# Transposing a second batch at full width: 96-row loads, copies and a new order in an attention and feed-forward kernel

## The chip, the cores and the metric

The kernel runs on one core of a Trainium2 chip. The metric is the device time of one execution in microseconds (us); less is better. Times shown are medians over executions, with their lowest and highest.

The core has a matrix engine (TensorE, PE in the profile, with its weight loads listed as PEld), a vector engine (VectorE, DVE), a scalar engine for activation functions (ScalarE, ACT), a general engine (GpSimd, POOL) and a queue engine (SyncE, SP). Matmuls read SBUF and write PSUM; a matmul holds one operand as weights in the array and streams the columns of the other through it. DMAs are issued from the queues of SP, ACT and POOL.

## The reference

```python
# q, k, v: [8 batches, 8 heads, 576, 64], f32; moe_w_in: [512, 2048]; moe_w_out: [2048, 512]
scores = (1 / sqrt(64)) * q @ k.transpose(0, 1, 3, 2)
mask = abs(pos[:, None] - pos[None, :]) <= 32
scores = where(mask, scores, -1e9)
attn = exp(scores - max(scores, -1))
attn = attn / (sum(attn, -1) + 1e-09)
x = (attn @ v).transpose(0, 2, 1, 3).reshape(8 * 576, 512)
h = x @ moe_w_in
out = maximum(0.01 * h, h) @ moe_w_out        # [4608, 512], f32
```

## The kernel before

The attention is cut into 64 steps. Step i belongs to batch b = i // 8, to half hf = (i // 4) % 2 of its 576 positions (288 each) and to a pair p = i % 4 of heads, whose 2 x 64 dimensions stand on the 128 partitions. A step is a set of scores (`score`: five matmuls into the one PSUM tile `ps`), an exponential on ACT (`exps`, tile `e`), the multiplication with the band mask (`masked`, tile `prob`, on POOL or DVE), the sums over keys (`sums`: matmuls with a block of ones, tile `s`), the reciprocal of the sums (`inverse`, a DVE instruction, tile `r`), the product with the values (`product`, tile `x`), and the scaling (`scaled`) into `xT`, the input of the feed-forward part. `sums` and `product` share a PSUM pool with one buffer for each of their tiles.

The feed-forward part goes by groups g of 288 positions: for each of 16 slices f of the hidden width `h_mms` makes four matmuls with `w_in_bf`, and ACT writes the leaky result to `gT` (`h_out`). For each 128 positions `o_tile` makes 16 matmuls of 512 columns with `w_out_bf`, in four groups of four with a hook before each; ACT copies the result out of PSUM and SP stores it.

The order on every engine is the order in which the program calls these functions (`manual_schedule`). The prologue, by hand, does steps 0 to 7 (batch 0) among the first feed-forward tiles. Then the loop at the end goes through a plan of hidden and output tiles; before each piece `spend` counts a turn, runs what the table `SECOND` lists for that turn, and later the steps that are due. `SECOND` covers batch 1's first half (steps 8 to 11) and the preparation of batch 2; turns 1 to 16 are the four groups of the first four output tiles.

What the change touches:

- Loading. `load_first` loads two heads side by side with a cast to bf16 onto 128 rows: 64 rows for each head of the pair, 9 positions of 64 in each row. It is used for batch 0 and, four times with two pairs each, for batch 1, issued from POOL's queue into `qb` and `kb`. POOL's queue also carries the weights (`load_w_in`, `load_w_out`, 512 KB each as bf16), batch 1's values (`load_v`), and in between POOL's own masks of steps 4, 5 and 6. A DMA on this queue waits for the one issued eight before it. The f32 loads of later batches (`load_qk`, tiles `qf` and `kf`, all pairs in `q_in` and `k_in`) go by SP.
- Transposing. For batches 0 and 1 `transpose_first` turns each head alone: 9 x 2 transposes of 64x64 into a PSUM tile `tp`, two quarters of the array at a time. `evict_first` copies `tp` to `qT` or `kT` on ACT or DVE; for the keys `place_keys` copies `kT` to block-diagonal `kbd` (two DVE copies). From batch 2 on, POOL casts the f32 rows (`cast_qk`) and a DMA transposes (`transpose_dma`); in the table these are `turned`. PSUM tiles `tp`, the hidden tiles and the output tiles share a pool of four buffers.
- Reciprocals. Steps 0 to 3 (`NEWTON`) do not use `inverse` but ACT's logarithm (`log_of`), ACT's exponential of its negative (`guess`), and one correction on DVE (`missed`, `mended`); `scaled` then takes the sign into account.

Of the kernel before, what the change touches and what calls it, by code (L numbers as in the profile page):

```python
# [10 lines left out]
BF16 = mybir.dt.bfloat16  # L11
# [5 lines left out]
def kernel(  # L17
# [14 lines left out]
    nc = tc.nc  # L32

    B, H, S, D = q.shape
# [5 lines left out]
    NPAIR = H // 2  # L40
# [17 lines left out]
    mmps = ctx.enter_context(tc.tile_pool(name="mmps", bufs=4, space=PS))  # L58
# [5 lines left out]
    RUN = S // 96  # L64
# [3 lines left out]
    q_in = fload.tile([128, H * RUN * D], FP32, name="qf")  # L68
    k_in = fload.tile([128, H * RUN * D], FP32, name="kf")

    def load_qk(b, p, behind=None):

        for into, src, t in ((qf, q, q_in), (kf, k, k_in)):
            t = t[0:96].rearrange("p (n a e) -> p n a e", n=NPAIR, a=2)[:, p]
            if behind is not None:
                behind.memset(t[0:1, 0, 0:1], 0.0)
                behind = None
            heads = src[b, 2 * p:2 * p + 2]
            nc.sync.dma_start(
                out=t.rearrange("p a (g e) -> p a g e", g=3),  # L80
                in_=heads.rearrange("a (g p c) d -> p a g (c d)", g=3, c=2),
            )
            into[b, p] = t

    ROW = S // 64
    qb_t = const.tile([128, NPAIR, RUN * 2 * D], BF16, name="qb")
    kb_t = const.tile([128, NPAIR, RUN * 2 * D], BF16, name="kb")
    qb, kb = (
        t[0:96].rearrange("i p (c a d) -> i p c a d", c=RUN, a=2) for t in (qb_t, kb_t)
    )  # L90
    q0b, k0b = (
        t[:, :, 0:ROW * D].rearrange("i p (c d) -> i p c d", c=ROW)
        for t in (qb_t, kb_t)
    )

    def load_first(b, p, which, n=1):

        src, to = ((q, q0b), (k, k0b))[which == "k"]
        nc.gpsimd.dma_start(
            out=to[:, p:p + n].rearrange("i p c d -> i p (c d)"),  # L100
            in_=src[b, 2 * p:2 * (p + n)].rearrange("(p a) (i c) d -> (a i) p (c d)", a=2, c=ROW),
        )
# [5 lines left out]
    def load_v(b, p, engs=(nc.sync, nc.sync)):  # L108
# [14 lines left out]
    ident = const.tile([128, 128], BF16)  # L123
# [6 lines left out]
        out=band, in_=band, compare_op=ALU.is_ge, fill=0.0,  # L130
# [3 lines left out]
        out=band, in_=band, compare_op=ALU.is_ge, fill=0.0,  # L134
# [16 lines left out]
    def copy_to(eng, out, in_):  # L151
        if eng is nc.scalar:
            eng.activation(out=out, in_=in_, func=AF.Copy)
        else:
            eng.tensor_copy(out=out, in_=in_)
# [45 lines left out]
    trans, kTs = {}, {}  # L201

    def transpose_first(b, p, which):

        src = (q0b, k0b)[which == "k"]
        tp = mmps.tile([128, ROW, 64], BF16, name="tp", tag="mm")
        for c in range(ROW):
            for r in HEADS:
                nc.tensor.transpose(tp[r, c], src[r, p, c], ident[r, r])  # L209
        trans[b, p, which] = tp.rearrange("p c i -> p i c")  # L210

    def evict_first(b, p, which, eng):
        if which == "q":
            if b not in qT:
                qT[b] = attn.tile([128, NPAIR, S], BF16, name="qT")
            to = qT[b][:, p]
        else:
            to = kTs[b, p] = kt.tile([128, S], BF16, name="kT")
        copy_to(eng, to.rearrange("p (i c) -> p i c", c=ROW), trans.pop((b, p, which)))

    def value_first(a, eng):
        r = HEADS[a]
# [29 lines left out]
    def place_keys():  # L252

        while landing and landing[0][0] <= state["done"]:
            unplaced.append(landing.pop(0)[1:])
        while unplaced:
            b, p, kT = unplaced.pop(0)
            for a in range(2):
                r = slice(64 * a, 64 * a + 64)
                to = kbd[b % 2][r, p, :, r]  # L260
                if b < NATURAL:
                    nc.vector.tensor_copy(out=to, in_=kT[r].rearrange("p (n j) -> p n j", j=64))
                    continue
                nc.vector.tensor_copy(  # L264
                    out=to.rearrange("p n (m c) -> p n c m", c=2),
                    in_=kT[r].rearrange("p (c n m) -> p n c m", c=2, n=NB),
                )
# [4 lines left out]
    def where(i):  # L272
        return i // 8, (i // 4) % 2, i % 4
# [43 lines left out]
    def masked(i, eng):  # L317
        b, hf, p = where(i)
        e = probs[i]
        pr = prob[:, i % NPROB]  # L320
        allowed = mask_first[hf] if b < NATURAL else mask[hf].rearrange("p n c i -> p n (c i)")
        eng.tensor_mul(  # L322
            pr.rearrange("p n c i -> p n (c i)"), e.rearrange("p (n t) -> p n t", n=2), allowed,
        )
        probs[i] = [pr, None, None, None]
# [9 lines left out]
    def sums(i, spare=False):  # L335

        b, hf, p = where(i)
        pr, both = probs[i][:2]
        if spare:
            s = mmps.tile([128, 512], FP32, name="mm", tag="mm")[:, 0:HALF]  # L340
        else:
            s = xps.tile([128, HALF], FP32, name="s")
        if both is not None:
            nc.tensor.matmul(s, ones_bd, both, start=True, stop=True)  # L344
        else:
            for n in range(2):
                nc.tensor.matmul(  # L347
                    s, ones_bd, pr[:, n].rearrange("p c i -> p (c i)"),
                    start=(n == 0), stop=(n == 1),
                )  # L350
        probs[i][2] = s
        if b > 0:
            inverse(i)

    def inverse(i):
        r = recip.tile([128, HALF], FP32, name="r")
        nc.vector.reciprocal(r, probs[i][2])  # L357
        probs[i][2] = r
# [10 lines left out]
    def missed(i):  # L369
        r = recip.tile([128, HALF], FP32, name="r")  # L370
        nc.vector.tensor_mul(r, probs[i][2], guesses[i])  # L371
        probs[i][2] = r
# [7 lines left out]
    def product(i):  # L380

        b, hf, p = where(i)
        pr = probs[i][0]
        x = xps.tile([128, HALF], FP32, name="x")
        x_v = x.rearrange("p (c i) -> p c i", c=2)
        flat = pr.rearrange("p n c i -> p n (c i)")
        parts = [(n_, *block) for n_ in range(2) for block in WIN[hf][n_]]
        for n_, blk, i0, n in parts:
            lo, hi = 2 * i0, 2 * (i0 + n)
            nc.tensor.matmul(  # L390
                x[:, lo:hi] if b < NATURAL else x_v[:, :, i0:i0 + n], vbd[b % 2][:, p, blk, :],
                flat[:, n_, lo:hi] if b < NATURAL else pr[:, n_, :, i0:i0 + n],
                start=(blk == parts[0][1]), stop=(blk == parts[-1][1]),
                skip_group_check=True,
            )
        probs[i][3] = x
# [4 lines left out]
        t0 = (b * S + hf * HALF) % RING  # L401
        return xT[:, p, t0:t0 + HALF]

    NEWTON = (0, 1, 2, 3,)

    def scaled(i):
        r, x = probs.pop(i)[2:]
        if i in NEWTON:
            nc.vector.scalar_tensor_tensor(  # L409
# [42 lines left out]
    def h_close(f):  # L452
        h_out(0, f, opened.pop(f))
# [99 lines left out]
    def load_w_out(i):  # L553
        c = slice(4 * i, 4 * i + 4)
        nc.gpsimd.dma_start(out=w_out_bf[:, c, :], in_=w_out_r[:, c, :])

    V, G, A = nc.vector, nc.gpsimd, nc.scalar
# [16 lines left out]
    exps(0)  # L574
    transpose_first(0, 1, "q")
    evict_first(0, 1, "k", A)
    masked(0, V)
    load_v(0, 2, (G, G))
# [56 lines left out]
    guess(3)  # L635
    h_chunk(1)
    masked(4, G)
    missed(3)
    score(5)
    product(3)  # L640
# [1 line left out]
    exps(5)  # L642
    h_chunk(2)
    scaled(3)
    load_w_out(3)
    sums(4)
    h_chunk(3)
    inverse(4)
    masked(5, G)
    product(4)  # L650
    h_close(0)
    score(6)
# [5 lines left out]
    h_close(2)  # L658
    sums(5)
    masked(6, G)  # L660
    load_first(1, 0, "k", 2)
    load_first(1, 0, "q", 2)
    load_first(1, 2, "k", 2)
    load_first(1, 2, "q", 2)
    score(7)
    h_close(4)
    inverse(5)
# [44 lines left out]
    for p in range(NPAIR):  # L712
        load_v(1, p, (G, G))
    for p in range(NPAIR):
        load_qk(2, p, G if p == 0 else None)

    def second_keys(p, eng):
        transpose_first(1, p, "k")
        evict_first(1, p, "k", eng)
        unplaced.append((1, p, kTs[1, p]))  # L720
        place_keys()

    def second_queries(p, eng):
        transpose_first(1, p, "q")
        evict_first(1, p, "q", eng)

    def finish(i):
# [3 lines left out]
    def turned(p):  # L731
        cast_qk(2, p)
        transpose_dma(2, p)

    SECOND = {
        1: [(second_keys, 0, A), (second_keys, 1, V)],
        3: [(second_queries, 0, A), (second_queries, 1, V)],
        4: [(second_keys, 2, A)],
        5: [(score, 8), (second_keys, 3, A)],
        6: [(score, 9)],  # L740
        7: [(sums, 8), (second_queries, 2, A), (second_queries, 3, A)],
        8: [(score, 10)],
        9: [(finish, 8), (sums, 9)],
        10: [(score, 11), (turned, 0)],
        11: [(finish, 9)],
        12: [(sums, 10), (turned, 1)],
        13: [(finish, 10)],
        14: [(score, 12), (turned, 2)],
        15: [(sums, 11)],
        16: [(finish, 11), (join, 12), (score, 13), (turned, 3)]  # L750
        + [(load_v, 2, p) for p in range(NPAIR)],
    }
    state["done"] = 12


# [11 lines left out]
    at, t = {}, 0.0  # L767
# [57 lines left out]
```

## Time and profile before

| | us |
|---|---|
| median of 3 runs | 315.47 |
| lowest, highest | 314.63, 315.93 |
| the profiled execution | 314.2 |
| its span | 312.5 |
| PE busy in the span | 304.2 |
| DVE, ACT, POOL busy | 218.7, 171.4, 177.9 |

The span is what the profile covers of the profiled execution; the rest lies around it. The granted PE clock is full in the whole span. Line numbers such as L209 are those of the kernel before, printed above. A row of the timeline reads: start, length, engine, line, operation, output<-input, shape, count, and in brackets the idle time before it with what ended it. PE's ends are modelled, and some matmul records are missing, so a group's time on PE is best read from its start to the start of the next group.

### The profile page before, as it was taken

The numbers are of one execution on the slowest core, as the hardware profiler recorded it, in microseconds if no ns is written. First come the engines' busy times: TensorE is split into PE (matmuls) and PEld (weight loads), VectorE is DVE, ScalarE is ACT, GpSimd is POOL, SyncE is SP. The second block draws the span as 40 slices with busy tenths as digits, with TensorE's granted clock in tenths as the row PEclk, the third lists the DMA queues.
The fourth block names the chain that finished last, engine by engine and source line by source line (L and its number), as shares of the span: only waits on it lengthen the run. The fifth ranks groups of instructions, "written<-read, shape, count | busy, mean of one in ns | idle before, by whom it ended". The sixth has DMA issues, their size and how long they took to land.

```text
span 312.5 us, 6890 instructions
## 1 busy us (share of the span) xinstructions
PE 304.2 (97%) x2662; PEld 205.7 (66%) x2683; DVE 218.7 (70%) x281; ACT 171.4 (55%) x380; POOL 177.9 (57%) x246
## 2 busy tenths in 40 slices
PE   5999999999999999999999999999999999999996
PEld 4777755776757667675856768585755858576753
DVE  6698588899557986699647996698665997665100
ACT  4775844664735556382825738283743828373531
POOL 8988625624648765686557855786456866330000
PEclk9999999999999999999999999999999999999999
DMA  7999999979999994699719994499627410000102
GB/s 123 171 199 207 206 188 226 218 139 225 227 181 213 244 196 103 157 222 171 157 42 212 213 216 112 115 224 222 141 63 126 109 56 34 36 35 5 65 30 73
DMA packets 107313, 46.09 MB, mean 147 GB/s; under 512 B 68752, under 2 KB 102800, under 8 KB 107280
## 3 DMA queue, kind: packets, MB, share of 16 engines
q1 hardware_dynamic: 91936, 37.91, 61.7%
q0 software_dynamic: 14752, 7.59, 18.3%
q8 instruction: 21, 0.34, 0.5%
q10 hardware_dynamic: 592, 0.15, 0.2%
q14 instruction: 12, 0.10, 0.1%
HBM read 36.70 MB, written 9.44 MB: 148 GB/s over the span
## 4 chain that ended last, share of the span: by engine, by line
PE 94%; DVE 2%; DMA 1%; issue 1%; ACT 1%; POOL 0%; DVEq 0%; ACTq 0%; POOLq 0%
PE mm L485 40%; PE mm L427 39%; PE x L390 5%; PE ps L303 4%; PE tp L209 2%; PE s L344 2%; DMA qb<-in_q_dram 1%; PE s L347 1%; PE ps L286 1%; DVE r L357 1%; PE ps L295 1%; DVE r L376 1%; DVE xT L409 0%; DVE r L371 0%; ACT e L314 0%
## 5 line engine op out<-in xcount | busy, mean ns | idle before, releaser
L357 DVE RECIPROCAL r<-s 128x288 f32<-128x288 f32 x60 | 117.4, 1956 | 52.3 <-PE s L344 50.3
L427 PE MATMUL mm<-xT,w_in_bf 128*128 128x288 bf16 x1024 | 133.8, 286 | 0.6 <-DVE xT L413 0.4
L485 PE MATMUL mm<-w_out_bf,gT 128*128 128x512 bf16 (+2 forms) x571 | 129.8, 373 | 1.2 <-issue 0.2
L438 ACT ACTIVATE gT<-mm 128x288 bf16<-128x288 f32 x256 | 101.7, 411 | 25.5 <-PE mm L427 8.9
L427 PEld LDWEIGHTS <-w_in_bf 128*128 128x128 bf16 x1024 | 98.5, 98 | 25.4 <-issue 1.2
L322 POOL TENSOR_TENSOR prob<-e,mask 128x576 bf16<-128x576 bf16 x48 | 61.2, 1274 | 84.3 <-issue 43.8
L485 PEld LDWEIGHTS <-gT 128*128 128x128 bf16 x592 | 55.9, 98 | 57.7
L490 ACT ACTIVATE o_sb<-mm 128x512 f32<-128x512 f32 (+2 forms) x37 | 21.7, 586 | 90.3 <-PE mm L485 87.2
L314 ACT ACTIVATE e<-ps 128x576 bf16<-128x576 f32 x64 | 41.4, 647 | 13.8 <-PE ps L303 7.4
L237 POOL CAST vbd<-vf 64x576 bf16<-64x576 f32 x48 | 32.8, 683 | 1.4
L264 DVE COPY kbd<-kT 64x576 bf16<-64x576 bf16 x48 | 32.4, 675 | 0.3
L413 DVE TENSOR_TENSOR xT<-x,r 128x288 bf16<-128x288 f32 x60 | 27.5, 458 | 6.4 <-DVE r L357 0.5
L232 POOL CAST kb<-kf 96x384 bf16<-96x384 f32 x48 | 27.5, 597 | 0.6 <-DMA kf<-in_k_dram 0.6
L232 POOL CAST qb<-qf 96x384 bf16<-96x384 f32 x48 | 24.6, 540 | 4.7 <-DMA qf<-in_q_dram 4.7
L390 PE MATMUL x<-prob,vbd 128*128 128x128 bf16 (+2 forms) x320 | 26.0, 213 | 0.0
L390 PEld LDWEIGHTS <-vbd 128*128 128x128 bf16 x320 | 20.3, 98 | 2.9
L332 DVE TENSOR_TENSOR both<-prob 128x288 bf16<-128x288 bf16 x52 | 19.8, 380 | 0.8
L303 PEld LDWEIGHTS <-kbd 128*128 128x128 bf16 x240 | 15.5, 98 | 6.7
L303 PE MATMUL ps<-qT,kbd 128*128 128x128 bf16 (+2 forms) x240 | 19.3, 211 | 0.0
L344 PE MATMUL s<-both,ones_bd 128*128 128x288 bf16 x52 | 14.9, 286 | 0.0
L115 POOL DMA_DIRECT2D vbd<-in_v_dram x14 | 10.4, 757 | 4.7 <-DMA kb<-in_k_dram 2.2
L322 DVE TENSOR_TENSOR prob<-e,wide 128x576 bf16<-128x576 bf16 x12 | 5.8, 485 | 4.1 <-ACT e L314 4.0
(57 smaller groups left out, 109.8 us busy)
## 6 DMA issues: line engine op xcount, KB each, us to landing
out_dram<-o_sb SPq DMA_DIRECT2D x35, 256.0 KB, 4.2
vf<-in_v_dram SPq DMA_DIRECT2D x49, 144.0 KB, 3.7
qf<-in_q_dram SPq DMA_DIRECT2D x24, 288.0 KB, 4.5
kf<-in_k_dram SPq DMA_DIRECT2D x24, 288.0 KB, 5.2
w_in_bf<-in_moe_w_in_dram POOLq DMA_DIRECT2D x4, 512.0 KB, 9.0
w_out_bf<-in_moe_w_out_dram POOLq DMA_DIRECT2D x4, 512.0 KB, 16.0
vbd<-in_v_dram POOLq DMA_DIRECT2D x14, 72.0 KB, 5.8
kb<-in_k_dram POOLq DMA_DIRECT2D x4, 144.0 KB, 4.6
```

Source lines behind the costliest of these rows:

```text
L232: nc.gpsimd.tensor_copy(out=dst[:, p, 3 * c:3 * c + 3], in_=by_c[c])
L237: nc.gpsimd.tensor_copy(out=vbd[b % 2][r, p, :, r], in_=vf[b, p][r])
L264: nc.vector.tensor_copy(out=to.rearrange("p n (m c) -> p n c m", c=2), in_=kT[r].rearrange("p (c n m) -> p n c m", c=2, n=NB),)
L303: nc.tensor.matmul(ps_v[:, n_, :, i0:i0 + n], kbd[b % 2][:, p, blk], by_c[:, :, hf * EVEN + i0:hf * EVEN + i0 + n], start=True, stop=True,)
L314: nc.scalar.activation(out=e, in_=ps[:, P0:P0 + 2 * HALF], func=AF.Exp, scale=scale)
L322: eng.tensor_mul(pr.rearrange("p n c i -> p n (c i)"), e.rearrange("p (n t) -> p n t", n=2), allowed,)
L357: nc.vector.reciprocal(r, probs[i][2])
L390: nc.tensor.matmul(x[:, lo:hi] if b < NATURAL else x_v[:, :, i0:i0 + n], vbd[b % 2][:, p, blk, :], flat[:, n_, lo:hi] if b < NATURAL else ...
L413: nc.vector.tensor_mul(place(i), x, r)
L427: nc.tensor.matmul(h[:, 0:HALF], w_in_bf[:, c, ts(f, 128)], xT[:, c, ds(g * HALF % RING, HALF)], start=(c == 0), stop=(c == DMC - 1),)
L438: nc.scalar.activation(out=to, in_=x, func=AF.Prelu, alpha=0.01)
L485: nc.tensor.matmul(o[:, lo:hi], gT[:, f, ds(128 * j % RING, 128)], w_out_bf[:, f, lo:hi], start=(f == 0), stop=(f == FFC - 1),)
```

## The change

Batch 1's queries and keys are loaded by `load_second` onto 96 rows, 6 positions of 64 in each row and for each head, so that the two heads of a pair lie apart in the row; the place is the second half of `q_in` and `k_in` read as bf16, where the f32 rows of pairs 2 and 3 of later batches go. `pair_up` copies a pair so that for each of the 6 positions the two heads stand side by side (96x768), on DVE or ACT. `transpose_second` then turns 96 rows by 128 columns at a time: 6 transposes on the whole array in place of 18 on quarters. Steps 8 to 11 join `NEWTON`. The loads are issued earlier on POOL's queue, two of them ahead of the last piece of `w_out`; batch 2's f32 loads of pairs 2 and 3 are moved into the table; and the table is written anew.

```diff
+    q1b, k1b = (
+        t[0:96].bitcast(BF16)[:, NPAIR * 2 * RUN * D:].rearrange("i (p a c d) -> i p a c d", p=NPAIR, a=2, c=RUN)
+        for t in (q_in, k_in)
+    )
+
+    def load_second(p, which, n):
+
+        src, to = ((q, q1b), (k, k1b))[which == "k"]
+        nc.gpsimd.dma_start(
+            out=to[:, p:p + n].rearrange("i p a c d -> i (p a) (c d)"),
+            in_=src[1, 2 * p:2 * (p + n)].rearrange("h (i c) d -> i h (c d)", c=RUN),
+        )
+
+    def pair_up(p, which, eng):
+
+        src, to = ((q1b, qb), (k1b, kb))[which == "k"]
+        copy_to(eng, to[:, p].rearrange("i c a d -> i a c d"), src[:, p])
...
+    def transpose_second(p, which):
+
+        src = (qb, kb)[which == "k"]
+        tp = mmps.tile([128, RUN, 96], BF16, name="tp", tag="mm")
+        for c in range(RUN):
+            nc.tensor.transpose(
+                tp[:, c], src[:, p, c].rearrange("i a d -> i (a d)"), ident[0:96, 0:96],
+            )
+        trans[1, p, which] = tp.rearrange("p c i -> p i c")
...
-        copy_to(eng, to.rearrange("p (i c) -> p i c", c=ROW), trans.pop((b, p, which)))
+        tp = trans.pop((b, p, which))
+        copy_to(eng, to.rearrange("p (i c) -> p i c", c=tp.shape[2]), tp)
...
-        if b > 0:
+        if b > 0 and i not in NEWTON:
             inverse(i)
+        elif b > 0:
+            for turn_ in (log_of, guess, missed, mended):
+                turn_(i)
...
-    NEWTON = (0, 1, 2, 3,)
+    NEWTON = (0, 1, 2, 3, 8, 9, 10, 11)
...
     masked(4, G)
+    load_second(0, "k", 2)
     missed(3)
...
     scaled(3)
-    load_w_out(3)
     sums(4)
...
     masked(5, G)
+    load_second(0, "q", 2)
+    load_w_out(3)
     product(4)
...
     masked(6, G)
-    load_first(1, 0, "k", 2)
-    load_first(1, 0, "q", 2)
-    load_first(1, 2, "k", 2)
-    load_first(1, 2, "q", 2)
+    load_second(2, "k", 2)
+    load_second(2, "q", 2)
     score(7)
...
     for p in range(NPAIR):
-        load_qk(2, p, G if p == 0 else None)
+        if p < 2:
+            load_qk(2, p, G if p == 0 else None)
...
+    def tk(p):
+        transpose_second(p, "k")
+
+    def ek(p, eng):
         evict_first(1, p, "k", eng)
         unplaced.append((1, p, kTs[1, p]))
-        place_keys()
...
     SECOND = {
-        1: [(second_keys, 0, A), (second_keys, 1, V)],
-        3: [(second_queries, 0, A), (second_queries, 1, V)],
-        4: [(second_keys, 2, A)],
-        5: [(score, 8), (second_keys, 3, A)],
-        6: [(score, 9)],
-        7: [(sums, 8), (second_queries, 2, A), (second_queries, 3, A)],
-        8: [(score, 10)],
-        9: [(finish, 8), (sums, 9)],
-        10: [(score, 11), (turned, 0)],
-        11: [(finish, 9)],
-        12: [(sums, 10), (turned, 1)],
-        13: [(finish, 10)],
-        14: [(score, 12), (turned, 2)],
-        15: [(sums, 11)],
-        16: [(finish, 11), (join, 12), (score, 13), (turned, 3)]
+        0: [(pair_up, 1, "q", V,), (pair_up, 0, "k", V,), (tq, 1,), (tk, 0,)],
+        1: [(ek, 0, A,), (pair_up, 1, "k", V,), (place_keys,)],
+        2: [(pair_up, 3, "k", V,)],
+        3: [(tk, 1,), (ek, 1, V,), (pair_up, 2, "q", V,), (place_keys,), (pair_up, 0, "q", A,), (eq, 1, A,)],
+        4: [(pair_up, 2, "k", A,), (pair_up, 3, "q", V,), (tq, 0,), (eq, 0, A,), (load_qk, 2, 3,)],
+        5: [(tk, 3,), (score, 8,), (tk, 2,), (ek, 2, A,), (tq, 2,)],
+        6: [(score, 9,), (eq, 2, A,), (ek, 3, A,), (place_keys,)],
+        7: [(sums, 8,), (tq, 3,)],
+        8: [(finish, 8,), (load_qk, 2, 2,), (score, 10,), (eq, 3, A,)],
+        10: [(turned, 0,), (sums, 9,), (score, 11,), (turned, 1,)],
+        12: [(finish, 9,), (score, 12,), (turned, 2,), (turned, 3,), (sums, 10,)],
+        14: [(finish, 10,)],
+        15: [(join, 12,), (sums, 11,)],
+        16: [(finish, 11,), (score, 13,)]
         + [(load_v, 2, p) for p in range(NPAIR)],
     }
+    for name, *args in SECOND.pop(0):
+        name(*args)
```

The names `tq` and `eq` do for the queries what `tk` and `ek` do for the keys. A and V are ACT and DVE.

More of the change, by code (lines that the diff above doesn't have):

```diff
@@ L714, with tq, eq @@
     for p in range(NPAIR):
-        load_qk(2, p, G if p == 0 else None)
-    def second_keys(p, eng):
-        transpose_first(1, p, "k")
+        if p < 2:
[3 more added lines that the diff above has]
+    def ek(p, eng):
         evict_first(1, p, "k", eng)
         unplaced.append((1, p, kTs[1, p]))
-        place_keys()
-    def second_queries(p, eng):
-        transpose_first(1, p, "q")
+    def tq(p):
+        transpose_second(p, "q")
+    def eq(p, eng):
         evict_first(1, p, "q", eng)
```

## The prediction

> **What bounds the kernel now.** I read the page first, then the waits of TensorE (PE), then PE's instructions in order of time through the stretch that the edits touch.
>
> ```profile
> span 312.5 us, 6890 instructions
> PE 304.2 (97%) x2662; PEld 205.7 (66%) x2683; DVE 218.7 (70%) x281; ACT 171.4 (55%) x380; POOL 177.9 (57%) x246
> PE 94%; DVE 2%; DMA 1%; issue 1%; ACT 1%; POOL 0%; DVEq 0%; ACTq 0%; POOLq 0%
> ...
> L357 DVE RECIPROCAL r<-s 128x288 f32<-128x288 f32 x60 | 117.4, 1956 | 52.3 <-PE s L344 50.3
> ```
>
> ```profile
> PE mm L427 <- DVE xT L413: 0.4, 1, 0.4
> ```
>
> PE is busy for 97% and carries 94% of the chain that ended last. The row above is PE's only wait on another engine after the first eight microseconds, 0.4 us, at 31. A reciprocal costs VectorE (DVE) 1.96 us, yet no PE row waits for one in the second batch. So an edit pays only if it takes columns or switches off PE, and costs only if it makes PE wait. PE in the stretch, each row a group (start, length up to the modelled end of its last instruction):
>
> ```profile
> 37.84 0.76 PE L209 MATMUL tp<-ident,kb 64*64 64x64 bf16 x36
> ...
> 40.36 0.76 PE L209 MATMUL tp<-ident,qb 64*64 64x64 bf16 x36
> 41.05 1.04 PE L485 MATMUL mm<-w_out_bf,gT 128*128 128x512 bf16 x4
> 42.02 0.47 PE L209 MATMUL tp<-ident,kb 64*64 64x64 bf16 x18
> 42.42 1.04 PE L485 MATMUL mm<-w_out_bf,gT 128*128 128x512 bf16 x3
> ...
> 44.90 0.40 PE L295 MATMUL ps<-qT,kbd 128*128 128x96 bf16 x5
> 45.14 1.03 PE L485 MATMUL mm<-w_out_bf,gT 128*128 128x512 bf16 x4
> 46.00 0.41 PE L347 MATMUL s<-prob,ones_bd 128*128 128x288 bf16 x2
> 46.34 0.75 PE L209 MATMUL tp<-ident,qb 64*64 64x64 bf16 x36
> 47.26 0.81 PE L485 MATMUL mm<-w_out_bf,gT 128*128 128x512 bf16 x3 [0.16 <-issue]
> ...
> 58.32 1.14 PE L427 MATMUL mm<-xT,w_in_bf 128*128 128x288 bf16 x8
> ```
>
> From 37.84 to 58.32 PE runs from group to group. Four matmuls of 512 columns take 0.86 (45.14 to 46.00), one set of scores 0.24 (44.90 to 45.14); by columns (0.216 per 512) two sum matmuls of 288 take 0.24. Where a group of four shows x3 (47.26), a record is missing, so that 0.16 is no wait.
>
> **The change, part by part.**
>
> *Transposes.* All 144 of 64x64 go, in eight sets of 18, which stand in five groups. From start to the next instruction's start a group of 36 takes 0.69 (40.36 to 41.05), one of 18 takes 0.40 (42.02 to 42.42): 0.29 per set and 0.11 on leaving a group. On entering, 0.10 is lost too: 41.05 plus 0.86 is 41.91, but the group starts at 42.02; 46.00 plus 0.24 is 46.24, but it starts at 46.34. The sum is 8 x 0.29 + 5 x 0.21 = 3.37 us; I take 3.35.
>
> Is the 0.21 of the transposes or of the small tiles? The prologue has scores in 64x64 tiles without a transpose:
>
> ```profile
> 17.34 1.14 PE L427 MATMUL mm<-xT,w_in_bf 128*128 128x288 bf16 x8
> 18.41 0.43 PE L286 MATMUL ps<-qT,kT 64*64 64x64 bf16 x10
> 18.77 0.41 PE L390 MATMUL x<-prob,vbd 128*128 128x96 bf16 x5
> ```
>
> Eight matmuls of 288 columns take 0.97, so 17.34 leads to 18.31, not 18.41: 0.10 on entering again. Its ten matmuls, in two concurrent halves, have the columns that take 0.24 in full tiles, but 0.36 pass: 0.12 on leaving. So it goes with the tile size, and full-array transposes should not pay it. The Trainium skill ("TensorEngine Tiling (Array Packing)", Key Properties) says that changing the tiling mode drains the array; by that rule the new groups pay nothing, and this trace agrees, with 0.10 and 0.12.
>
> Added: 8 x 6 transposes that load 96x128 as weights and stream 96 columns. No such row exists. The nearest is a set of scores: five matmuls of 96, 128, 64, 128 and 128 columns, each with a new weight tile, in 0.24; 0.44 ns a column, 42 ns for 96, so 2.0 us for 48. The bounds are the weight loads:
>
> ```profile
> L303 PEld LDWEIGHTS <-kbd 128*128 128x128 bf16 x240 | 15.5, 98 | 6.7
> ...
> L209 PE MATMUL tp<-ident,kb 64*64 64x64 bf16 x144 | 4.5, 217 | 0.4 <-DMA kb<-in_k_dram 0.4
> ...
> L209 PEld LDWEIGHTS <-kb 64*64 64x64 bf16 x144 | 3.7, 130 | 2.0 <-DMA kb<-in_k_dram 1.5 <-issue 0.4
> ```
>
> If each 98 ns load stood in the open, 48 would take 4.7 us. But 18 loads of 130 ns pass in 0.29, so loads overlap: I take 2.0. Net -1.35 (bounds -1.4 and +1.35).
>
> *Loads and POOL's queue.*
>
> ```profile
> 19.87 1.29 POOL L322 TENSOR_TENSOR prob<-e,wide 128x576 bf16<-128x576 bf16 x1
> 22.12 1.27 POOL L322 TENSOR_TENSOR prob<-e,wide 128x576 bf16<-128x576 bf16 x1 [0.97 <-ACT e L314]
> ...
> 36.58 0.73 POOL L115 DMA_DIRECT2D vbd<-in_v_dram  x1 [1.67 <-DMA w_out_bf<-in_moe_w_out_dram]
> 38.10 0.73 POOL L115 DMA_DIRECT2D vbd<-in_v_dram  x1 [0.79 <-DMA kb<-in_k_dram]
> 39.28 0.73 POOL L115 DMA_DIRECT2D vbd<-in_v_dram  x1 [0.46 <-DMA qb<-in_q_dram]
> 41.39 1.53 POOL L115 DMA_DIRECT2D vbd<-in_v_dram  x2 [1.38 <-DMA kb<-in_k_dram]
> ```
>
> ```profile
> 25.14 0.41 PE L347 MATMUL s<-prob,ones_bd 128*128 128x288 bf16 x2
> ```
>
> Step 6's mask (22.12) now has two issues ahead of it: free at 21.16, plus two issues at the 0.73 to 0.77 of the rows below it is 22.7, 0.6 later, done at 24.0; its sums start on PE at 25.14, so nothing waits. Cover gone, the price is that 0.6. Behind it POOL issues the second batch's last two loads, by about 27, when the queue is still 7 us from serving them. The last four POOL rows show when loads had landed: last part of w_out 36.6, keys of pairs 0 and 1 38.1, their queries 39.3, keys of pairs 2 and 3 41.4. The queue is served in order of issue and saturated:
>
> ```profile
> 36.00:38.00 2.00, 2.00 (x26) 1.44 (x26) 0.00 (x0) 1.68 (x5) 0.73 (x1) 1.00 1.22 208
> ```
>
> At 208 GB/s 512 KB take 2.5 us. The two loads of pairs 0 and 1 pass ahead of that piece: keys at 35.6, queries at 36.8; w_out's last at 39.3 (its matmuls come near 41.5); the rest as before: keys of pairs 2 and 3 at 41.4, their queries by 42.2. The rows are 768 bytes written instead of 1152; if packets and not bytes counted, each load would take up to 1.5 times as long, 0.7 more.
>
> *Copies and the new waits.* The eight copies of 96x768 have no row. Nearest:
>
> ```profile
> 31.11 4.79 DVE L708 MEMSET kbd<- 128x576 uint32 x8
> L262 DVE COPY kbd<-kT 64x576 bf16<-64x576 bf16 x8 | 3.6, 447 | 4.1 <-ACT kT L153 3.9
> ...
> L153 ACT ACTIVATE kT<-tp 128x576 bf16<-128x576 bf16 x5 | 3.3, 652 | 1.0 <-PE tp L209 1.0
> ...
> L155 DVE COPY kT<-tp 128x576 bf16<-128x576 bf16 x3 | 2.3, 758 | 1.1 <-PE tp L209 1.0
> ```
>
> By width, DVE 0.60 (bounds 0.45, and 1.0 by the copy that reads PSUM), ScalarE (ACT) 0.87 (0.65 to 0.87). DVE is free at 35.9 and waits for the queries at 36.8: pair 1's queries are copied by 37.4, pair 0's keys by 38.0, where PE's first two sets (from 37.75) want them: up to 0.1 lost. The long wait is the keys of pair 2, on ACT's queue: it holds ACT until 41.4, the copy ends by 42.25, and queued behind it stands the eviction of pair 0's queries (0.65, to 42.9), for which step 8's scores wait on PE. Five sets and four groups of 512 columns, 1.25 + 3.45, stand before them, so PE is there at 37.75 + 4.7 + 0.1 = 42.55: about 0.3 lost. On DVE, pair 3's keys at 41.4 to 42.0 are just in time for their set at 42.3. After that each product, score and sum comes with its inputs 0.2 us or more ahead by the same addition. Waits: +0.4 (bounds 0, and 1.6 if both the landing and the copies are at their worst).
>
> *Reciprocals 8 to 11.* Four times 1.96 leave DVE; 0.45 + 0.46 and, on ACT, 0.41 + 0.44 take the place:
>
> ```profile
> 15.74 0.40 ACT L364 ACTIVATE y<-mm 128x288 f32<-128x288 f32 x1
> 16.18 0.44 ACT L367 ACTIVATE y<-y 128x288 f32<-128x288 f32 x1
> 16.68 0.45 DVE L371 TENSOR_TENSOR r<-mm,y 128x288 f32<-128x288 f32 x1
> 17.16 0.46 DVE L376 SCALAR_TENSOR_TENSOR r<-r,y 128x288 f32<-128x288 f32 x1
> ```
>
> 15.74 to 17.62 is 1.9 us, as late as a reciprocal: nothing gained on PE. Before, none was waited for; the products stand 8 matmuls (1.7 us) behind their sums. Cost 0; with that cover gone, what stands ahead on ACT, 0.65 an eviction, for each.
>
> *SP.* The third batch's loads of pairs 2 and 3 move behind the copies that free their space, and the first output's store behind the load of pair 3, which waits for a copy near 44.4.
>
> ```profile
> 50.25 2.03 SPq L491 DMA_DIRECT2D out_dram<-o_sb  x2
> ```
>
> ```profile
> 57.16 0.94 POOL L232 CAST qb<-qf 96x384 bf16<-96x384 f32 x2
> ```
>
> The store was issued at 50.25, behind eight loads, and stands behind six now. The casts of pairs 2 and 3 stood behind step 12's mask (57.16), which now comes some 3 us sooner, so loads that land by 57 are in time: cost 0; one late transpose would cost its lateness at step 18.
>
> *Sum.* -1.35 + 0.4 = -0.95. The profiled execution took 314.2 (312.5 of it span): 313.25. It lies 1.27 under the median 315.47 of the runs shown, which gives **314.5**.
>
> **Rivals.**
> - *The loads or ACT's queue eat it.* For: everything waits on 41.4. Against: 0.3 is all I find. With waits at 1.3 the time is 315.4, no change.
> - *The change does not take the switches off PE*: a transpose pays its 0.21 at full size too. Six groups remain: +1.25, 315.8. Against: the L286 rows.
> - *The weight loads do not hide* (slower): 96 rows of weights into 128 columns, 98 ns each: +1.4 + 0.4, 317.3. The gain is gone at 61 ns a load. Against: full tiles run at column speed.
> - *Each transpose runs its whole length alone*, 217 ns as the L209 row has it: 48 x 0.217 - 3.35 + 0.4 = +7.5, 323.0. Against: 18 of these pass in 0.29. The Trainium skill ("TensorE: Matmul & The Clock Gate", Part 4: PE-mode transpose) gives about 275 ns for a 128x128 transpose inside one kernel; read as a spacing that would be an estimated 13.2 us for 48. The trace's 0.29 contradicts such a reading.
> - *No wait arises*, and the lighter DVE brings step 12 on sooner: -1.4 and up to 0.3 of small gaps, 313.8.
>
> **How the numbers follow.** Chances: forecast 0.50 (its own range 313.9 to 315.2), eaten gain 0.17, switches stay 0.09, loads in the open 0.13, whole lengths 0.01, no wait 0.10. The range 313.4 to 316.9 leaves out the two last slow cases in good part and the ends. Runs of this kernel differ by 1.3 us, so under 0.5% (1.6 us, 313.9 to 317.0) a change cannot be told from none. Faster needs 313.9: a fifth of the forecast and most of the last case, 0.18. Slower: nearly all of the loads in the open, whole lengths and a little of the rest, 0.17. Same: 0.65.
>
> **What would show it.** Right: 48 transposes some 42 ns apart with no 0.1 before or after; the h matmuls that started at 58.32 start near 57.4; the one new PE wait is at step 8's scores, some 0.3, on ACT's qT. Wrong: transposes 98 ns or more apart; PE waiting for DVE's copy of the first queries; any PE wait for products 9 to 11, which would be the logarithms behind ACT's evictions.

## The result, and the profile after

| | before | changed |
|---|---|---|
| median of 20 runs each, us | 315.06 | 313.81 |
| lowest, highest | 314.11, 316.9 | 312.77, 316.05 |
| ratio of the times, 95% interval | | 0.9961 [0.9947, 0.9976] |
| the profiled execution, its span | 314.2, 312.5 | 312.77, 311.1 |

The changed kernel is 0.4% faster (0.24 to 0.53%). That is less than the 0.5% set as the bound of "the same" in the prediction, so the case of highest chance came in. The interval leaves out 1: with twenty runs of each kernel this change can be told from none, though the prediction held that under 0.5% it could not. The time lies inside the range, 0.7 under the 314.5 forecast, and at the 313.8 of the rival "no wait arises", which had a chance of 0.10. Of the 0.7, 0.4 is the kernel before: the forecast counted from the 315.47 of three runs, and twenty runs gave 315.06.

PE's timeline in the changed kernel, through the stretch that the prediction shows of before (start, length, group of instructions):

```profile
28.61 0.40 PE L422 MATMUL x<-prob,vbd 128*128 128x64 bf16 x5
28.85 1.69 PE L459 MATMUL mm<-xT,w_in_bf 128*128 128x288 bf16 x12
30.89 6.82 PE L459 MATMUL mm<-xT,w_in_bf 128*128 128x288 bf16 x52 [0.36 <-DVE xT L445]
37.55 0.42 PE L235 MATMUL tp<-ident,qb 96*128 96x96 bf16 x6
37.81 0.42 PE L235 MATMUL tp<-ident,kb 96*128 96x96 bf16 x6
38.07 1.89 PE L517 MATMUL mm<-w_out_bf,gT 128*128 128x512 bf16 x7
...
40.92 0.42 PE L235 MATMUL tp<-ident,qb 96*128 96x96 bf16 x6
41.17 1.03 PE L517 MATMUL mm<-w_out_bf,gT 128*128 128x512 bf16 x4
42.04 0.42 PE L235 MATMUL tp<-ident,kb 96*128 96x96 bf16 x6
42.30 0.41 PE L324 MATMUL ps<-qT,kbd 128*128 128x96 bf16 x5
...
56.80 1.14 PE L459 MATMUL mm<-xT,w_in_bf 128*128 128x288 bf16 x8
```

A set of six transposes takes 0.25 to 0.26 from its start to the next (37.55 to 37.81, 40.92 to 41.17), that is 42 to 43 ns from one transpose to the next. Nothing is lost around it: the four matmuls of 512 columns from 41.17 end 0.86 later at 42.03, and the next set starts at 42.04. Step 8's scores start 0.26 after that set, without a wait.

The measure used below is the stretch from the start of the h matmuls that wait for `xT` of step 7 to the first h matmuls of the next group: before 31.09 to 58.32, 27.23 us; now 30.89 to 56.80, 25.91 us. So 1.32 us are gained in it. Before it the changed kernel is 0.20 ahead, which is chance (changed_again and loads_alone below). Behind it nothing is gained: from 58.32 to the span's end at 312.5 it was 254.2 us before, and from 56.80 to 311.1 it is 254.3 now.

### The profile page after: what moved, and what is told of

Same layout as the page of the kernel before. It is cut to its first block, busy times and chain, and to the rows that moved or that the text cites. A ratio compares the mean times of both kernels' runs of the same rounds, so it can differ in the third digit from the quotient of the medians.

```text
span 311.1 us, 6722 instructions
## 1 busy us (share of the span) xinstructions
PE 302.1 (97%) x2566; PEld 205.0 (66%) x2587; DVE 216.6 (70%) x290; ACT 176.0 (57%) x391; POOL 178.5 (57%) x246
## 4 chain that ended last, share of the span: by engine, by line
PE 93%; DVE 2%; DMA 1%; issue 1%; ACT 1%; POOL 0%; ACTq 0%; DVEq 0%; POOLq 0%
PE mm L459 40%; PE mm L517 40%; PE x L422 5%; PE ps L332 4%; PE s L373 2%; DMA qb<-in_q_dram 1%; PE s L376 1%; PE tp L235 1%; DVE r L389 1%; PE ps L324 1%; DVE prob L351 1%; PE ps L315 1%; PE tp L227 0%; ACT e L343 0%; DVE r L408 0%
## 5 line engine op out<-in xcount | busy, mean ns | idle before, releaser
L389 DVE RECIPROCAL r<-s 128x288 f32<-128x288 f32 x56 | 109.6, 1957 | 50.3 <-PE s L373 49.5
L343 ACT ACTIVATE e<-ps 128x576 bf16<-128x576 f32 x64 | 41.4, 646 | 11.9 <-PE ps L332 7.4
L445 DVE TENSOR_TENSOR xT<-x,r 128x288 bf16<-128x288 f32 x56 | 25.7, 458 | 5.8
```

Of the source, the lines that this page charges most:

```text
L343: nc.scalar.activation(out=e, in_=ps[:, P0:P0 + 2 * HALF], func=AF.Exp, scale=scale)
L445: nc.vector.tensor_mul(place(i), x, r)
```

## The experiments

The ratios are to the kernel before, run on the same chip in the same comparison; its median was 314.85 to 315.25 there, so kernels of different comparisons are set side by side by their ratios, and these are not exactly quotients of the medians shown. The last column but one shows where the stretch begins and ends in the profile of that kernel.

| kernel | median us | ratio [95% interval] | stretch, from and to | us |
|---|---|---|---|---|
| before | 315.06 | 1 | 31.09, 58.32 | 27.23 |
| changed | 313.81 | 0.9961 [0.9947, 0.9976] | 30.89, 56.80 | 25.91 |
| changed_again | 313.92 | 0.9971 [0.9951, 0.9991] | 31.37, 57.27 | 25.90 |
| log_alone | 315.29 | 1.0010 [0.9996, 1.0023] | 32.20, 59.45 | 27.25 |
| no_log | 314.69 | 0.9995 [0.9981, 1.0008] | 31.32, 58.13 | 26.81 |
| loads_alone | 314.88 | 1.0001 [0.9988, 1.0013] | 31.52, 58.74 | 27.22 |
| layout_alone | 322.93 | 1.0253 [1.0212, 1.0294] | 31.41, 64.45 | 33.04 |
| late_loads | 315.41 | 0.9999 [0.9985, 1.0014] | 31.95, 59.46 | 27.51 |
| small_tiles | 316.03 | 1.0045 [1.0024, 1.0065] | 30.99, 58.91 | 27.92 |
| full_tiles | 314.91 | 0.9997 [0.9979, 1.0016] | 31.89, 58.48 | 26.59 |
| act_held | 315.06 | 1.0004 [0.9984, 1.0025] | 31.72, 58.96 | 27.24 |

**The changed kernel once more: changed_again.**

> The changed kernel once more, for its time beside the next two and for the spread of the prologue. Theory (the gain is the 1.32 us between the h matmuls of the two groups; the start of the first of these groups, 30.9 to 32.2 in the profiled runs so far, differs by chance): ratio 0.996 and the stretch from there to the next group 25.9 again, whatever the start. Rival (0.2 of the gain belongs to the prologue): the group starts near 30.9 again.

The stretch is 25.90 again, and it starts at 31.37, later than in the kernel before. So the gain of the change is in the stretch, and the 0.20 ahead of it in the first pair of profiles was chance.

**One part of the change alone: log_alone and loads_alone.** The first is the kernel before with this edit (and the branch in `sums` that goes with it):

```diff
-    NEWTON = (0, 1, 2, 3,)
+    NEWTON = (0, 1, 2, 3, 8, 9, 10, 11)
```

> The kernel before with one edit: reciprocals of steps 8 to 11 by logarithm. Theory (the whole gain of the change is columns and tile switches of TensorE, 1.33 us; the rest only keeps its inputs in time): no PE row waits for a reciprocal in the second batch before, so the time stays at 315.1 within 0.3, and the h matmuls of the second group start where they started before, 58.3, but for what the prologue brings. Rival (the lighter VectorE gives part of the gain): 314.5 or less, those matmuls by 57.8.

Its ratio holds 1 and its stretch is 27.25: the logarithms by themselves bring nothing. The h matmuls of the second group start later than the expectation says (59.45), because the prologue was 1.1 later in this run; the stretch leaves that out.

The second moves the loads of pairs 0 and 1 in the kernel before:

```diff
     masked(4, G)
+    load_first(1, 0, "k", 2)
...
     masked(5, G)
+    load_first(1, 0, "q", 2)
+    load_w_out(3)
```

> The kernel before with one edit: the second batch's loads of pairs 0 and 1 issued where the change issues them, ahead of the last part of w_out. Theory: PE did not wait for these loads before, so 315.1 within 0.3. The 0.2 us by which the changed kernel's PE was ahead at 31 was then chance of the prologue. Rival (the new places of the loads give that 0.2 by themselves, by moving the steps of POOL's masks): 314.8 and the group at 31.09 starting at 30.9 again; a second rival is a loss, the mask of step 6 coming 0.6 later: 315.7.

Ratio 1.0001, stretch 27.22, and a start at 31.52, not 30.9. The rival falls: the 0.2 at the beginning does not come with the loads. In the profiles of the table this start lies anywhere between 30.9 and 32.2.

**The logarithms taken out again: no_log.** The changed kernel with `NEWTON` as it was before.

> The changed kernel with reciprocals again in steps 8 to 11. Theory: the new order lets the logarithm matter. VectorE would hold the reciprocal of step 8 from 47.3 to 49.2 where the new order has the sums of step 9 on PE at 48.6, and these need the same one PSUM buffer, so PE waits some 0.6 there, and the like may follow at steps 10 and 11: 313.8 + 0.6 to 1.5, that is 314.4 to 315.3. Rival (the logarithms do nothing in the new order either): 313.8 within 0.3 and no new PE wait.

Its stretch is 0.90 longer than the changed kernel's. PE's waits and PE's and DVE's timeline in no_log:

```profile
PE s L376 <- DVE r L389: 0.5, 1, 0.5
```

```profile
45.84 1.84 DVE L291 COPY kbd<-kT 64x576 bf16<-64x576 bf16 x4
47.71 1.96 DVE L389 RECIPROCAL r<-s 128x288 f32<-128x288 f32 x1
...
50.61 1.94 DVE L389 RECIPROCAL r<-s 128x288 f32<-128x288 f32 x1
```

```profile
47.29 1.89 PE L517 MATMUL mm<-w_out_bf,gT 128*128 128x512 bf16 x8
49.72 0.41 PE L376 MATMUL s<-prob,ones_bd 128*128 128x288 bf16 x2 [0.54 <-DVE r L389]
...
52.16 0.40 PE L324 MATMUL ps<-qT,kbd 128*128 128x64 bf16 x5
52.61 0.41 PE L376 MATMUL s<-prob,ones_bd 128*128 128x288 bf16 x2
```

The reciprocal of step 8 starts only when four block-diagonal copies are done, and the sums of step 9 need the buffer that it reads. Eight matmuls from 47.29 end at 49.02 (8 x 0.216), so PE stands for 0.70 by starts (the row of the waits has 0.5 and the timeline 0.54, with PE's ends modelled). The second reciprocal ends at 52.55, and the sums of step 10 start at 52.61, 0.21 later than the 0.24 of the scores ahead of them would let them. 0.70 + 0.21 is 0.91, the 0.90 within rounding. So the same edit is worth nothing in the old order and 0.9 us in the new one.

**The layout in the old order: layout_alone.** The changed kernel's loads of 96 rows, copies (all on DVE, each just ahead of its set) and full-size transposes, with the loads' places, the reciprocals and the rest of the table as before (batch 2's f32 loads of pairs 2 and 3 come in turn 8).

```diff
+        1: [(pair_up, 0, "k", V), (pair_up, 1, "k", V), (second_keys, 0, A), (second_keys, 1, V)],
+        3: [(pair_up, 0, "q", V), (pair_up, 1, "q", V), (second_queries, 0, A), (second_queries, 1, V)],
+        4: [(pair_up, 2, "k", V), (second_keys, 2, A)],
+        5: [(score, 8), (pair_up, 3, "k", V), (second_keys, 3, A)],
...
+        7: [(sums, 8), (pair_up, 2, "q", V), (pair_up, 3, "q", V), (second_queries, 2, A), (second_queries, 3, A)],
```

> The changed kernel with the layout, the copies and the full-size transposes, but with the loads, the reciprocals and the order of the work as they were before. Theory: the 1.33 us of PE are saved here too, but PE now waits for the copies: 0.5 at the first set, because the keys land near 37.7 and their copy takes 0.36, and 1 or more at the first queries, whose copies stand on VectorE behind the block-diagonal copies of pair 1: 315.0 to 316.5. Rival (the order was not needed): 313.8 within 0.3 and no PE wait on a copy.

It is slower by more than the theory said: 7.1 us over the changed kernel in the stretch, where 1.2 to 2.7 was expected in the time. The wait expected at the first set did not come; by starts, four later waits at sets of transposes are 2.0, 0.4, 1.9 and 2.4, together 6.8. PE and then DVE in layout_alone:

```profile
42.34 0.70 PE L235 MATMUL tp<-ident,qb 96*128 96x96 bf16 x12 [1.87 <-DVE qb L173]
...
47.43 0.43 PE L235 MATMUL tp<-ident,kb 96*128 96x96 bf16 x6 [1.75 <-DVE kb L173]
...
52.34 1.00 PE L235 MATMUL tp<-ident,qb 96*128 96x96 bf16 x12 [2.26 <-DVE qb L173]
```

```profile
46.65 0.46 DVE L351 TENSOR_TENSOR prob<-e,wide 128x576 bf16<-128x576 bf16 x1 [0.45 <-ACT e L343]
47.03 0.35 DVE L173 COPY kb<-kf 96x768 bf16<-96x768 bf16 x1
...
50.11 1.96 DVE L389 RECIPROCAL r<-s 128x288 f32<-128x288 f32 x1
51.98 0.86 DVE L173 COPY qb<-qf 96x768 bf16<-96x768 bf16 x2
```

From the first queries on, the short copies stand in DVE's queue behind instructions that themselves depend on PE: the keys of pair 3 behind the mask of step 8, the last queries behind the reciprocal of step 8. So PE's transposes wait for DVE, which waits for what PE did just before. That is what the new order takes apart, by putting most copies groups ahead of their sets and two of the eight on ACT. How much of the 7.1 us the table alone is worth was not run: late_loads below and no_log account for 1.6 and 0.9 in the new order, and that the rest is the table's is argued, not shown. The median is 9.1 us over the changed kernel's, more than this profile shows; its runs went from 320.43 to 325.04, and what the longer ones lost was not seen.

**The loads in their old place: late_loads.** The changed kernel with `load_w_out(3)` first and the four loads of `load_second` together behind step 6's mask.

> The changed kernel with the loads of pairs 0 and 1 behind the last part of w_out, keys first, all in one place as before. Theory: the queries of pair 1, which PE wants first at 37.55, land near 38.5 and are copied in 0.36, and PE waits 1.3 (1.0 to 1.8) at the first set and nowhere else: 313.7 + 1.3 = 315.0. Rival (the loads' places do nothing here, as they did nothing in the kernel before): 313.7 within 0.3.

PE in late_loads:

```profile
40.19 0.43 PE L235 MATMUL tp<-ident,qb 96*128 96x96 bf16 x6 [1.43 <-DVE qb L173]
```

One wait of 1.43 at the first set, the stretch 1.60 longer, and 1.5 us more than changed_again in the same comparison (315.41 against 313.92). The loads' new place, worth nothing in the kernel before, is what the new order stands on.

**The price of a change of tile size: small_tiles and full_tiles.** Each set gets two transposes more, once of 64x64 and once of full size:

```diff
         tp = mmps.tile([128, RUN, 96], BF16, name="tp", tag="mm")
+        for r in HEADS:
+            nc.tensor.transpose(tp[r, 0, 0:64], ident[r, r], ident[r, r])
```

> The changed kernel with one pair of 64x64 transposes of the identity ahead of each of the eight sets, into PSUM that the set then overwrites (16 instructions more). Theory (changing the tile size costs 0.10 on entering and 0.11 on leaving, whatever the number of small tiles): each pair costs 0.21 + 0.03, so 8 x 0.24 = 1.9, from the start of the h matmuls at 31 to those of the next group 25.9 + 1.9 = 27.8, and 313.6 + 1.9 = 315.5. Rival (the 0.21 went with something else in the old groups): 8 x 0.03 = 0.3, that is 313.9.

> The changed kernel with two full-size transposes more ahead of each of the eight sets (the same 16 instructions, but of 96 rows by 128 columns). Theory (no switch, 42.5 ns each, weight loads hidden): 16 x 0.0425 = 0.7, the stretch 26.6, 314.3: less than the 64x64 pairs cost, though each full transpose moves more columns. Rival (weight loads in the open): 16 x 0.098 = 1.6, 315.2.

PE in small_tiles, then in full_tiles:

```profile
40.49 0.22 PE L235 MATMUL tp<-ident 64*64 64x64 bf16 x2
40.64 0.43 PE L237 MATMUL tp<-ident,kb 96*128 96x96 bf16 x6
40.90 1.03 PE L519 MATMUL mm<-w_out_bf,gT 128*128 128x512 bf16 x4
41.86 0.22 PE L235 MATMUL tp<-ident 64*64 64x64 bf16 x2
```

```profile
40.96 0.25 PE L235 MATMUL tp<-ident,kb 96*128 96x96 bf16 x2
41.05 0.42 PE L237 MATMUL tp<-ident,kb 96*128 96x96 bf16 x6
41.30 1.03 PE L519 MATMUL mm<-w_out_bf,gT 128*128 128x512 bf16 x4
42.17 0.25 PE L235 MATMUL tp<-ident,qb 96*128 96x96 bf16 x2
```

In small_tiles the matmuls from 40.90 take 0.86, but the small pair starts 0.96 later, at 41.86: 0.10 on entering. The pair and the way back take 0.15 (40.49 to 40.64). Eight of these are 2.0, and the stretch grew by 2.01 (1.9 expected). In full_tiles the same group takes 0.87 to the next start, each transpose adds 0.0425 or so, and the stretch grew by 0.68 (0.7 expected). Sixteen instructions cost three times as much on the small tiles, and it is the change that is paid for. The Trainium skill ("TensorEngine Tiling (Array Packing)", Key Properties) says that a change of mode drains TensorE; these runs put a price on a pair of changes here: 0.25 with one pair of transposes in it.

**The wait that was predicted and did not come: act_held.** `(pair_up, 2, "k", A,)` stands three times in turn 4.

> The changed kernel with the copy of pair 2's keys made three times on ScalarE, which holds it until about 42.3 as the prediction had it by a landing at 41.4. Theory (the predicted wait was a right chain with a landing 1.4 too late): the copies run from 40.1 to 42.35, the eviction of pair 0's queries ends at 43.0 instead of 42.0, and PE, which is at step 8's scores at 42.3, waits 0.7 there and nowhere else: the stretch 26.6, 314.3. Rival (ScalarE's queue was never in the way): 313.6 within 0.3 and no PE wait.

ACT and PE in act_held:

```profile
41.28 2.60 ACT L171 ACTIVATE kb<-kf 96x768 bf16<-96x768 bf16 x3 [0.28 <-DMA kf<-in_k_dram]
43.78 0.63 ACT L171 ACTIVATE qT<-tp 128x576 bf16<-128x576 bf16 x1
```

```profile
42.86 0.42 PE L235 MATMUL tp<-ident,kb 96*128 96x96 bf16 x6
44.46 0.40 PE L324 MATMUL ps<-qT,kbd 128*128 128x96 bf16 x5 [1.18 <-ACT qT L171]
```

The chain is as predicted: keys of pair 2, ACT's copy, the eviction of pair 0's queries behind it, PE at step 8's scores, and no other new wait. It cost 1.33 instead of 0.7: in this run the keys landed at 41.28, 1.2 later than the expectation had the copies start, and the copies took 2.60, not 2.25, while PE was only 0.8 later than in the changed kernel's profile. An estimate from these rows: with one copy the eviction would have ended near 42.8 (41.28 + 0.84 + 0.65), before PE came at 43.12. Here the keys are about as late as predicted, but PE's first set is too (38.38, where the prediction had 37.75), and so there would have been no wait.

**A version beyond the change: sums_sooner, both_sooner, copies_moved.** In the changed kernel PE loses time twice more in this part: 0.36 or more for `xT` of step 7 (row 30.89 above), and some 0.3 among the 52 h matmuls behind it, which take 6.66 (30.89 to 37.55) where 0.122 each would make 6.3. There the fifth h tile needs a PSUM buffer that ACT has not emptied yet. sums_sooner moves `sums(7)` and `inverse(7)` ahead of `h_open(14)`. both_sooner also gives that fifth tile the buffer of `s`:

```diff
+        if (g, f) == (1, 4):
+            hs = [xps.tile([128, HALF], FP32, name="s")]
```

copies_moved, on top, turns pair 0's keys first and copies pair 2's keys on DVE.

> The changed kernel with the sums and the reciprocal of step 7 one group of h matmuls sooner. PE has one wait on another engine left between 9 and 300 us, 0.36 for xT of step 7 at 30.9, and VectorE idles 0.41 ahead of that reciprocal. Theory: the reciprocal starts 0.41 sooner and PE gains about 0.4: 313.2, ratio 0.9948. Rival (VectorE is held elsewhere, or PE's start of the next group is not what counts): 313.6 as the changed kernel, ratio 0.996.

> The changed kernel with the sums and the reciprocal of step 7 one group of h matmuls sooner (sums_sooner) and the fifth h tile of the second group in the PSUM buffer of the sums, which is free there, so that PE no longer stands for 0.29 until ScalarE has emptied the first. Theory: 0.49 + 0.29 off the path, from the start of product 7 to the h matmuls of the next group 28.2 - 0.8 = 27.4 us, and about 0.8 less than the changed kernel in the same comparison: ratio near 0.9937. Rival (the fifth tile's wait only moves on to the sixth): 27.7, ratio 0.9948.

> The kernel both_sooner with two copies moved: pair 2's keys are copied on VectorE, no longer ahead of the eviction of pair 0's queries on ScalarE, and the first set of transposes is that of pair 0's keys, which land before pair 1's queries. In both_sooner PE, by then 0.7 earlier, waited 0.26 at the first set and 0.26 ahead of step 8's scores, for ScalarE stood from 41.0 to 41.9 until pair 2's keys had landed: the chain that the prediction had priced at 0.3. Theory: both waits go, from the start of product 7 to the h matmuls of the next group 27.4 to 27.5 us, 313.2 - 0.4 = 312.9 or ratio 0.993. Rival (the loads are late for VectorE's other copies as well, and PE waits for pair 2's or 3's keys in place of it): 28.0, ratio 0.994 as both_sooner.

| kernel | median us | ratio [95% interval] | product 7 to next group's h | us |
|---|---|---|---|---|
| changed | 313.81 | 0.9961 [0.9947, 0.9976] | 28.61, 56.80 | 28.19 |
| changed_again | 313.92 | 0.9971 [0.9951, 0.9991] | 29.09, 57.27 | 28.18 |
| sums_sooner | 313.82 | 0.9975 [0.9951, 1.0000] | 29.65, 57.35 | 27.70 |
| both_sooner | 313.33 | 0.9941 [0.9923, 0.9960] | 29.80, 57.83 | 28.03 |
| copies_moved | 313.88 | 0.9970 [0.9945, 0.9994] | 29.93, 57.56 | 27.63 |

By the profiles sums_sooner takes 0.49 off this part. The fifth tile's buffer was the right one: 64 h matmuls and what stands between them take 8.21 to the first set in sums_sooner (29.89 to 38.10) and 7.92 in copies_moved (30.17 to 38.09). In both_sooner most came back: 0.36 ahead of the first set (8.28, 30.04 to 38.32; the profile puts 0.19 of it down to DVE's copy of pair 1's queries), and then this. Its ACT and PE:

```profile
41.90 0.84 ACT L171 ACTIVATE kb<-kf 96x768 bf16<-96x768 bf16 x1 [0.93 <-DMA kf<-in_k_dram]
42.65 0.63 ACT L171 ACTIVATE qT<-tp 128x576 bf16<-128x576 bf16 x1
```

```profile
42.83 0.42 PE L235 MATMUL tp<-ident,kb 96*128 96x96 bf16 x6
43.33 0.40 PE L324 MATMUL ps<-qT,kbd 128*128 128x96 bf16 x5
```

The scores start 0.50 after the set instead of 0.26. ACT stood for pair 2's keys until 41.90: here, with the landing 3.6 behind PE's first set (41.90 and 38.32) and not 2.4 as in the changed kernel's profile (39.96 and 37.55), is the predicted wait, at 0.24. copies_moved takes it away (27.63), though 0.2 appears at pair 2's queries. In the times none of this is established: all the intervals overlap, both_sooner is 0.6 us under changed_again in one comparison, and copies_moved, with the shortest stretch, is not faster (in its profiled run PE had waited 1.62 for weights in the prologue). Whether one of them beats the changed kernel stays open.

## Why the prediction was right, and where it was not

- *Transposes: -1.35 predicted, -1.32 measured.* 48 at 42 to 43 ns (42 predicted) with their weight loads hidden, and no loss on entering or leaving; 3.37 taken off less 48 x 0.0425 added is the 1.33. That it fits this closely is better than the prediction could know, whose bounds for the added transposes went up to 4.7 us. The rivals "switches stay", "loads in the open" and "whole lengths" fall with the rows of L235; small_tiles and full_tiles confirm the price of a switch and that it goes with the tile size.
- *Waits: +0.4 predicted, 0 measured. This is the term that was off.* The chain was right (act_held, both_sooner), its lateness was not. Two sizes failed. The landing of the keys of pairs 2 and 3 was put at 41.4, where POOL resumed before; but a row of POOL's is only an upper bound. In the changed kernel DVE works on these keys at 39.96 and POOL resumes at 40.46, and in the seven profiles in which DVE stands for this load, it starts 0.50 or 0.51 ahead of POOL's row. The prediction's own lines could have shown it: PE turns the keys of pairs 0 and 1 from 37.84, POOL resumes for them at 38.10. The second size is DVE's copy, 0.36 where the lower bound was 0.45, so the 0.1 at the first set fell away.
- *That the wait is 0 and not small is in part luck.* In the profiled execution of the changed kernel ACT evicted pair 0's queries from 41.37 and was done at 42.02, 0.28 before PE came at 42.30; PE's own transposes, not the keys, had set that start. In changed_again, the same kernel, ACT does stand for pair 2's keys until 41.03, evicts from 41.85 to 42.50, and PE comes at 42.77: the predicted chain, 0.27 short of a wait.
- *The rival "no wait arises"* had the time, but not its second half: no small gaps closed behind step 12 (254.2 and 254.3 us). Without them it would have stood at 314.1; that it meets 313.81 is the luck of a kernel before that came out 0.4 lower. By the same luck the time lies under the 313.9 that the prediction asked of a faster kernel, while the ratio says the same.
- *The signs.* The transposes came 42 to 43 ns apart with no 0.1 around them, and no sign of being wrong appeared. The next group's h matmuls started at 56.80, not 57.4, and the wait at step 8's scores did not come.
- *Reciprocals: 0* holds for the order before (log_alone). The prediction took it as a property of the edit. In the new order it is the condition for the rest (no_log, 0.9): "before, none was waited for" does not carry over to an order that puts copies ahead of the first reciprocal.
- *SP, the mask of step 6, casts: 0.* Nothing of these shows on PE.

POOL, DVE and ACT in the changed kernel, then POOL, DVE, ACT and PE in changed_again:

```profile
40.46 0.73 POOL L133 DMA_DIRECT2D vbd<-in_v_dram  x1 [1.02 <-DMA kf<-in_k_dram]
```

```profile
36.01 0.36 DVE L173 COPY qb<-qf 96x768 bf16<-96x768 bf16 x1 [0.31 <-DMA qf<-in_q_dram]
...
39.96 0.36 DVE L173 COPY kb<-kf 96x768 bf16<-96x768 bf16 x1
```

```profile
40.08 0.84 ACT L171 ACTIVATE kb<-kf 96x768 bf16<-96x768 bf16 x1
41.37 0.65 ACT L171 ACTIVATE qT<-tp 128x576 bf16<-128x576 bf16 x1 [0.46 <-PE tp L235]
```

```profile
41.54 0.73 POOL L133 DMA_DIRECT2D vbd<-in_v_dram  x1 [0.98 <-DMA kf<-in_k_dram]
```

```profile
41.03 0.36 DVE L173 COPY kb<-kf 96x768 bf16<-96x768 bf16 x1 [0.70 <-DMA kf<-in_k_dram]
```

```profile
41.03 0.84 ACT L171 ACTIVATE kb<-kf 96x768 bf16<-96x768 bf16 x1 [0.38 <-DMA kf<-in_k_dram]
41.85 0.65 ACT L171 ACTIVATE qT<-tp 128x576 bf16<-128x576 bf16 x1
```

```profile
42.77 0.40 PE L324 MATMUL ps<-qT,kbd 128*128 128x96 bf16 x5
```

The queries of pairs 0 and 1 were expected at 36.8 and copied from 36.01 here, but from 37.12 in changed_again, still ahead of PE's first set at 38.03. From run to run the landing of the keys of pairs 2 and 3 moves: 39.96 or sooner here, 41.03 in changed_again, 41.28 in act_held, 41.90 in both_sooner; PE's first set moves too, but not by as much. One trace gives one draw of it, and a forecast of 0.3 for a wait that hangs on it could have been 0 as well.

## What to carry to other kernels

When an engine is busy for 97%, price an edit by what it takes off that engine, switches of its mode included; that part came out within 0.03 us here. Then ask of the order what it needs: here two edits that are worth 0 in the old order (loads, logarithms) and the new table carry a gain of 1.3 us; with all three left out, the layout is a loss of several us. A wait that is sized from a DMA's landing should be taken with the spread between runs, and a row that only resumes after a landing is a bound, not the landing.

## What the runs showed of the hardware

*A DVE instruction stood still while POOL multiplied.* The correction of step 3's reciprocal has its two inputs in SBUF and takes 0.46 elsewhere. In the kernel before and in both_sooner (DVE's and POOL's rows each):

```profile
18.58 0.85 DVE L376 SCALAR_TENSOR_TENSOR r<-r,y 128x288 f32<-128x288 f32 x1
```

```profile
17.81 1.29 POOL L322 TENSOR_TENSOR prob<-e,wide 128x576 bf16<-128x576 bf16 x1
```

```profile
18.50 1.85 DVE L408 SCALAR_TENSOR_TENSOR r<-r,y 128x288 f32<-128x288 f32 x1
```

```profile
18.75 1.28 POOL L351 TENSOR_TENSOR prob<-e,wide 128x576 bf16<-128x576 bf16 x1
```

POOL's mask ends at 19.10 and 20.03, DVE's instruction at 19.43 and 20.35: 0.32 to 0.33 later both times. In the changed kernel it overlaps the mask by only 0.17 and takes 0.48. In log_alone and copies_moved it is over before the mask starts (from 18.84 and 18.04, the mask from 19.53 and 19.54), and it takes 0.46. The Trainium skill ("SBUF — State Buffer", Who interferes with whom) says that a VectorE instruction with two inputs in SBUF and a GpSimd instruction that reads SBUF exclude each other; the rows agree, though in both_sooner DVE's row starts 0.25 ahead of POOL's and still ends behind it. Whether this makes the 0.2 by which the profiles of the kernel before and the changed one differ ahead of the stretch is not shown, and it does not explain the wider spread: log_alone, without the overlap, starts the stretch latest of all, at 32.20.

*The quick copy.* 768 elements a row took 0.36 on DVE, while a block-diagonal copy of 576 takes 0.45 (the row of L262 in the prediction). The Trainium skill ("VectorE: DVE Perf Modes", What auto-detection actually checks) says that the engine chooses a faster mode by itself, by the type of the operands, where they lie and their outer dimensions. Which of these sets the two copies apart no run here tried. The prediction scaled the narrower copy by its width to 0.60 and took its 0.45 as the lower bound; the wider copy is quicker than either.
